# An S4D long convolution and a gMLP block on one core: inverse transforms in other matrix tiles, and a first phase in a new order

## Chip, cores and metric

One core of one Trainium2 chip. The metric is the device time of one execution in microseconds, the median of several runs.

## What is computed

The reference, cut to what matters (L = 2048 positions, D = 512 channels, N = 128 states a channel, Fh = 896):

```python
def _A_ref(u, log_A_real, A_imag, C_real, C_imag, log_dt, D_skip):
    dt = jnp.exp(log_dt)
    A = -jnp.exp(log_A_real) + 1j * A_imag
    C = (C_real + 1j * C_imag) * dt[:, None]
    P = jnp.exp((A * dt[:, None])[:, :, None] * pos[None, None, :])
    K = 2.0 * jnp.einsum("dn,dnl->dl", C, P).real
    y = irfft(rfft(u_t, 2 * L) * rfft(K, 2 * L)[None], 2 * L)[:, :, :L]
    return y.transpose(0, 2, 1) + u * D_skip[None, None, :]

def _B_ref(x, w_in, w_sp, b_sp, w_out):
    z = gelu(einsum("bsd,df->bsf", x, w_in))
    z1, z2 = z[..., :Fh], layernorm(z[..., Fh:])
    g = einsum("ts,bsf->btf", w_sp, z2) + b_sp[None, :, None]
    return einsum("bsf,fd->bsd", z1 * g, w_out)

h = x + _A_ref(layernorm(x), ...)
return h + _B_ref(layernorm(h), ...)
```

## The kernel before

The engines are TensorE (PE, with its weight loads as PEld), VectorE (DVE), ScalarE (ACT), GpSimd (POOL) and SyncE (SP), which issues most DMA transfers. A matmul in float32 shows as two records of MATMUL and two of LDWEIGHTS; "records" below are those of MATMUL.

**First phase (`phase_a`, 0 to 305 us of the span).** The channels are worked in four chunks of 128. `params` turns the parameters of a chunk into magnitudes and phases, on small tiles in buffers called `trio`; each phase is split in three parts that stand six rows above another six of them, and all rows of a chunk go to a scratch in HBM (`scr_stk`) in 16 stores of 16x6x128 a chunk. Four further rows of ones (`marks`) are written there once, by two transfers. `stack` reloads half a chunk as `sw` (512 KB), in the layout that TensorE needs. `unit` (8 a chunk) makes the kernel K of 16 channels: matmuls `c_k` x `sw` give all phases, ACT takes their sine, VectorE and GpSimd multiply them with powers (`f`, `wa`), and many small matmuls (`product`, 32x64 tiles) sum over the states into `ks`.

The long convolution is a transform of 4096 points in two stages, done as matmuls, for x and for K: `piece_a` and `piece_c` are the first stage (`st1`, 64x64 tiles, named `wb,big` and `wb,ks` in the profile), `piece_b` and `piece_d` the second (the matrix `a2`, shown as `big,a`); `piece_d` also multiplies the two spectra on VectorE; `exchange` swaps halves of partitions by DMA (`trio<-trio`). `piece_e` is the first stage of the inverse. For each of 4 channels it issues 8 matmuls with 64-column stationaries and 64 moving columns, 32 in a piece, 1024 in all; its result goes to `big`, with real and imaginary part on the two halves of the partitions.

The order of all this is written as tables. `RANKS` gives each operation its place, `FORMS` says for each operation that two engines could do which one does it (`evac`, the copy out of PSUM, is on ACT or VectorE), and `BANKS` gives each result its PSUM bank. All of it is recorded through one helper, so that every instruction of this phase has line 253. Within its engine an instruction waits behind whatever the table puts ahead of it; loads and stores stand in the same order on SP's queue.

**Second phase (`phase_b1`, 305 to 403 us).** It ends the inverse transform and begins the gMLP. `lines(n, g)` (matmul line 757) makes four lines of positions of quarter n, group g, as `y<-big,g`: 8 matmuls with 128 rows and 64 columns, two column tiles side by side, 16 groups in all. The matrix `g` is a constant of 2 MB. Group results of quarter 0 are added to x straight out of PSUM on VectorE (`add`, line 772), those of quarters 1 to 3 are first copied to a `stash` by ACT (`put_by`, line 764) and added later (line 769). `moments` (776), `centre` (matmul 785, called pm), `spread` (matmul 799, called pv), `scaled` (822 and 824), `turned` (831, 833) and `lower` (837) normalize and transpose 512 positions into `ht`; `by_halves` does that for quarter 0 in two halves; `column` (matmul 875) multiplies with `w_in`. `w1r` is `w_in` as loaded, split into high and low parts at 693 and 694. y, pz and the like share seven PSUM banks in turn; a new one waits until its bank's last content was copied away. The order on the engines is that of the calls at the end of the function.

**Afterwards** come the other half of `w_in` (`phase_b2`, 403 to 480 us) and the spatial product, the gate and the output (`phase_b3`, 480 to 839.7 us), which the change does not touch.

## Time and profile before

| | |
|---|---|
| median of 3 runs | 842.04 us (839.42 to 848.31) |
| the profiled execution | 841.47 us, span 839.7 |
| first phase | 0 to 305.14 us |
| last 512 records of `piece_e` | from 289.95 us |
| first y of the second phase | 305.78 us |
| DMA traffic | 121.22 MB, 144 GB/s on average |
| stores of `scr_stk`, reload of `sw` | 512.0 KB a reload, 8 reloads, 4.6 us to landing |

The span is the time between the first and the last record of the profile; the execution's own time is 1.8 us longer. A row of instructions names the line, the engine, the operation and output<-input, the shape, and how many. "Idle before" is time in which an engine waited, with the engine, tile and line that released it. Busy shares are averages over stages with different limits, so that the profile is read by stages: the busy time of each engine in a window, then the waits that end in it.

### The profile page before, as it was taken

How to read it: one execution, taken by the hardware profiler on the slowest of the kernel's cores; microseconds unless marked ns; L12 is line 12 of the kernel's file. 1: busy time of each engine (PE TensorE's matmuls, PEld its weight loads, DVE VectorE, ACT ScalarE, POOL GpSimd, SP SyncE). 2: the span in 40 equal slices, each digit the busy share in tenths (PEclk: the TensorE clock that was granted, in tenths of full speed). 3: DMA queues.
4: the chain of work that ended last, by engine and by line, in shares of the span. 5: the costliest groups of instructions: out<-in, count | busy, mean ns of one | idle time of the engine just before them, and what ended most of it. 6: DMA issues, size and time to landing. Idle time of an engine off the chain costs nothing.

```text
span 839.7 us, 22552 instructions
## 1 busy us (share of the span) xinstructions
PE 770.3 (92%) x9361; PEld 657.0 (78%) x9361; DVE 603.3 (72%) x1172; ACT 441.6 (53%) x778; POOL 285.1 (34%) x339
## 2 busy tenths in 40 slices
PE   1288898898898799999999999999999999999998
PEld 1157788787797699788999988888888888888887
DVE  7898597586676468764367689988956984888533
ACT  5889588688675145555224354466444443454111
POOL 4799599867745000000042100233231002232200
PEclk9999899899999999999999999999999999999999
DMA  9515442430505816545164044999799458799632
GB/s 339 159 36 156 119 103 70 110 84 26 129 4 108 335 19 174 139 138 188 39 151 125 1 139 140 193 231 219 186 207 214 156 148 203 159 246 243 153 110 79
DMA packets 70007, 121.22 MB, mean 144 GB/s; under 512 B 7569, under 2 KB 25105, under 8 KB 68881
## 3 DMA queue, kind: packets, MB, share of 16 engines
q1 hardware_dynamic: 58240, 98.28, 38.7%
q0 software_dynamic: 11664, 21.50, 15.6%
q8 instruction: 73, 1.20, 0.6%
q14 instruction: 30, 0.24, 0.1%
HBM read 90.40 MB, written 22.02 MB: 134 GB/s over the span
## 4 chain that ended last, share of the span: by engine, by line
PE 63%; DVE 1%; ACT 1%; issue 0%
PE m L1186 33%; PE pz L981 9%; PE pz L875 8%; PE po L1109 7%; PE pl L1109 2%; PE ps L253 2%; PE y L757 1%; DVE stats L776 0%; ACT w1r L824 0%; DVE xq L772 0%; ACT ht L833 0%; PE lnh_pm L785 0%; PE lnh_pv L799 0%; ACT zo L878 0%; ACT big L253 0%
## 5 line engine op out<-in xcount | busy, mean ns | idle before, releaser
L1186 PE MATMUL m<-wts,zc_wa 128*128 128x512 f32 x700 | 221.0, 395 | 0.0
L1186 PEld LDWEIGHTS m<-wts,zc_wa 128*128 128x128 f32 x700 | 131.7, 188 | 31.0
L1186 PE MATMUL m<-wts,zc_wb 128*128 128x512 f32 x350 | 138.0, 394 | 0.0
L1057 POOL DMA_DIRECT2D raws<-in_w_sp_dram x64 | 58.2, 1018 | 213.0 <-DMA raws<-in_w_sp_dram 212.2
L253 POOL TENSOR_TENSOR wa<-mt 128x512 f32<-128x512 f32 x96 | 107.2, 1138 | 26.8 <-PE ps L253 16.2
L693 ACT CAST wts<-raws 128x512 fp32r<-128x512 f32 x112 | 69.0, 619 | 47.6 <-DMA raws<-in_w_sp_dram 21.1
L694 DVE TENSOR_TENSOR wts<-raws,wts 128x512 fp32r<-128x512 f32 x112 | 76.7, 687 | 15.2 <-ACT wts L693 15.1
L1186 PEld LDWEIGHTS m<-wts,zc_wb 128*128 128x128 f32 x350 | 65.8, 188 | 15.6
L981 PE MATMUL pz<-w,ht 128*128 128x448 f32 x384 | 77.0, 362 | 0.0
L981 PEld LDWEIGHTS pz<-w,ht 128*128 128x128 f32 x384 | 72.0, 187 | 4.9
L875 PE MATMUL pz<-ht,w1h 128*128 128x512 f32 (+1 forms) x248 | 73.3, 376 | 0.1
L253 PE MATMUL ps<-c_inv,trio 128*64 128x64 f32 x2048 | 63.4, 224 | 3.2 <-DVE trio L253 2.2
L987 POOL TENSOR_SCALAR sm<-sm 128x1 f32<-128x1 f32 x16 | 5.6, 347 | 178.0 <-DVE sm L986 178.0
L253 PEld LDWEIGHTS ps<-c_inv,trio 128*64 128x64 f32 x2048 | 61.9, 140 | 4.8 <-DVE trio L253 2.6
L1109 PE MATMUL po<-w,gz 128*128 128x512 f32 x252 | 61.7, 392 | 0.0
L693 ACT CAST zc_wa<-raws 128x384 fp32r<-128x384 f32 (+1 forms) x70 | 37.1, 533 | 45.3 <-DVE raws L1091 24.3
L253 PE MATMUL ps<-big,a 128*128 128x128 f32 x448 | 56.1, 286 | 1.7 <-DVE trio L253 1.0
L253 PEld LDWEIGHTS ps<-big,a 128*128 128x128 f32 x448 | 54.5, 200 | 3.6 <-DVE trio L253 1.3
L1109 PEld LDWEIGHTS po<-w,gz 128*128 128x128 f32 x252 | 47.3, 188 | 10.7
L253 DVE TENSOR_TENSOR f<-ps,wa 128x512 f32<-128x512 f32 (+1 forms) x64 | 46.8, 750 | 8.6 <-ACT ps L253 4.1
L875 PEld LDWEIGHTS pz<-ht,w1h 128*128 128x128 f32 x248 | 45.1, 188 | 9.5 <-ACT ht L833 0.5
L253 DVE COPY big<-ps 128x512 f32<-128x512 f32 x39 | 26.1, 687 | 30.9 <-PE ps L253 30.8
(170 smaller groups left out, 1440.0 us busy)
## 6 DMA issues: line engine op xcount, KB each, us to landing
raws<-in_w_sp_dram SPq DMA_DIRECT2D x112, 256.0 KB, 4.0
raws<-in_w_sp_dram POOLq DMA_DIRECT2D x80, 256.0 KB, 5.9
trio<-trio SPq DMA_DIRECT2D x32, 256.0 KB, 3.8
scr_z<-zo SPq DMA_DIRECT2D x28, 256.0 KB, 2.0
big<-in_u_a_dram SPq DMA_DIRECT2D x8, 512.0 KB, 7.1
sw<-scr_stk SPq DMA_DIRECT2D x8, 512.0 KB, 4.6
xq<-in_u_b_dram SPq DMA_DIRECT2D x4, 1024.0 KB, 6.9
scr_h<-xq SPq DMA_DIRECT2D x16, 256.0 KB, 4.8
```

The source lines that it names most:

```text
L253: r = getattr(getattr(self.nc, e), method)(*map(self.real, args), **{k: self.real(x) for k, x in kw.items()})
L693: nc.scalar.copy(hi, src)
L694: nc.vector.tensor_sub(lo, src, hi.bitcast(F32))
L757: nc.tensor.matmul(ys[n, g][64 * h:64 * h + 64, i, :], gt[:, l0 + i], qv[:, h, l0 + i], start=True, stop=True, tile_position=(0, 64 * h))
L875: nc.tensor.matmul(pt[:, w], a[:, q, f], ht[n][k][:, q, w], start=((q, i) == terms[0]), stop=((q, i) == terms[-1]))
L981: nc.tensor.matmul(pt[:, :FQ], a[:, q], w2[:, b, q, f], start=(q == 0 and i == 0), stop=(q == 3 and i == 2))
L987: nc.gpsimd.tensor_scalar_add(sm[:, 14:15], sm[:, 13:14], 1e-5)
L1057: nc.gpsimd.dma_start(r, ws[1], accum_op=ALU.add)
L1109: nc.tensor.matmul(pt, gz[fb][x][:, P * a:P * a + P], wo[:, y, fb, w], start=(first and fb == fbs[0] and i == 0), stop=(last and fb == fbs ...
L1186: nc.tensor.matmul(pt, x[:, f], y, start=(k == 0 and i == 0), stop=(k == KT - 1 and i == 2))
```

## The change

1. `piece_e` uses stationaries of 128 columns and moves 128 columns: 2 matmuls for a channel, 8 a piece, 256 in all. Its result in `big` has the two halves of the points on the partitions and real and imaginary part along the free axis.
2. `lines` follows: it sums over real and imaginary part in two matmuls of 64x64 tiles, two groups at a time, 32 matmuls a pair of groups, 256 in all (128 before). In quarter 0 only the two tiles on the diagonal are used in turn; in quarters 1 to 3 all four, with even and odd lines on the two halves of the partitions. Rows of one half write a PSUM bank of their own. `g` becomes a constant of 4 MB in four pieces of 1 MB; two are loaded with the other early loads, two when the first phase's buffers are free.
3. `put_by` sorts even and odd lines with two copies of 64 partitions in place of one of 128: 24 copies, before 12. The calls of the second phase stand in a new order.
4. `stk` has the layout that the stores have, [4, 2, 64, 16, 128]: 4 stores a chunk in place of 16; `marks` takes four transfers; the reload reads runs of 512 bytes where it read 2 KB.
5. `RANKS`, `FORMS` and `BANKS` are new throughout the first phase. By engine: copies into `trio` go from 27 on ACT and 5 on VectorE to 18 and 14; the table loads on ACT from 15 to 20.

```diff
-    g = np.zeros((P, NL2, 64))
+    g = np.zeros((2, 64, NL2, 2, 64))
...
-        g[:, q] = np.einsum("ikl,qr->ikqrl", t, np.eye(2)).reshape(P, 64)
-    c["c_g"] = g.reshape(P, NL2 * 64)
+        g[:, :, q] = np.einsum("ikl,qr->kqirl", t, np.eye(2)).reshape(64, 2, 64)
+    c["c_g"] = g.reshape(P, NL2 * 128)
...
-    sws = [one(g1, f"sw{h}", [2, 4, NS]) for h in range(2)]
+    sws = [one(g1, f"sw{h}", [4, 2, NS]) for h in range(2)]
...
-    marks = stk_d.rearrange("c h (i r) s n -> (c h i) (r s n)", r=16)[:, 6 * 4 * NS:10 * 4 * NS]
-    for w in (slice(0, 32), slice(32, 128)):
-        nc.sync.dma_start(marks[w], cst["c_one"].to_broadcast([w.stop - w.start, 16 * NS]))
+    marks = stk_d.rearrange("c h p r n -> (c h p) r n")[:, 6:10]
+    for c in range(NCH):
+        nc.sync.dma_start(marks[P * c:P * c + P], cst["c_one"].rearrange("o (r n) -> o r n", r=4).to_broadcast([P, 4, NS]))
...
-            for su in range(SUC):
-                d = stk_d[c0 + c, su // 4].rearrange("(i r) s n -> s i r n", r=16)[su % 4]
+            for h in range(2):
                 for r in (0, 10):
-                    nc.sync.dma_start(d[:, r:r + 6], st6[16 * su:16 * su + 16, :, c, :])
+                    nc.sync.dma_start(stk_d[c0 + c, h, :, r:r + 6], st6[64 * h:64 * h + 64, :, c, :])
...
-        nc.sync.dma_start(sws[h], stk_d[c, h].rearrange("(a p) s n -> p a s n", a=2))
+        nc.sync.dma_start(sws[h], stk_d[c, h].rearrange("(s a i) r n -> (i r) s a n", s=4, a=2))
...
             for dd in range(4):
-                for h in range(2):
-                    for i, t in enumerate(spectra(c)[:2]):
-                        for r in range(2):
-                            nc.tensor.matmul(pt[64 * r:64 * r + 64, dd, 64 * h:64 * h + 64], t[:, 4 * s + dd, h],
-                                             c_inv[:, P * i + 64 * r:P * i + 64 * r + 64], start=(i == 0), stop=(i == 1),
-                                             tile_position=(0, 64 * r))
+                for i, t in enumerate(spectra(c)[:2]):
+                    nc.tensor.matmul(pt[:, dd, :], t[:, 4 * s + dd], c_inv[:, P * i:P * i + P], start=(i == 0), stop=(i == 1))
...
-    def lines(n, g, part=range(4)):
...
+    def lines(n, *groups):
+        for g in groups:
+            ys[n, g] = bank(f"y{n}_{g}", [P, 4, P])
+        if n == 0:
+            for turn in range(2):
+                for i in range(4):
+                    for r in range(2):
+                        for x, g in enumerate(groups):
+                            h, l = turn ^ x, 4 * g + i
+                            w = slice(64 * h, 64 * h + 64)
+                            nc.tensor.matmul(ys[n, g][w, i, :], gs[n][w, l, r], qv[w, r, l], start=(r == 0), stop=(r == 1),
+                                             tile_position=(64 * h, 64 * h))
+            return
+        for i in range(4):
+            for r in range(2):
+                for h, g in enumerate(groups):
+                    for odd in range(2):
+                        w, o, l = slice(64 * h, 64 * h + 64), 64 * odd, 4 * groups[0] + 2 * i + odd
+                        nc.tensor.matmul(ys[n, g][o:o + 64, i, :], gs[n][w, l, r], qv[w, r, 16 * n + l], start=(r == 0),
+                                         stop=(r == 1), tile_position=(64 * h, o))
+
+    for n, tag in ((2, "h21"), (3, "h11")):
+        gs.append(hp.tile([P, 16, 2, 64], F32, tag=tag, name=f"g{n}"))
+        load_g(n)
...
     def put_by(n, g):
-        o = stash[n][:, g].rearrange("p (l d x) -> p l d x", l=4, d=4)
-        nc.scalar.copy(o, ys[n, g].rearrange("p l (x d) -> p l d x", d=4))
+        h, y = g % 2, ys[n, g].rearrange("p l (x d) -> p l d x", d=4)
+        o = stash[n][:, g - h:g - h + 2].rearrange("p g (l d x) -> p (g l) d x", l=4, d=4)
+        for odd in range(2):
+            nc.scalar.copy(o[64 * h:64 * h + 64, odd::2], y[64 * odd:64 * odd + 64])
...
             scaled(n, 2 * h + 1)
-            if h:
-                put_by(2, 3)
             turned(n, 2 * h)
...
+            if h == 0:
+                put_by(2, 0)
+                put_by(2, 1)
...
-        lines(2, 0)
-        put_by(2, 0)
+        lines(2, 0, 1)
         add(1, 0)
         root(0, spread(0))
-        for n, g in ((2, 1), (2, 2), (2, 3), (3, 0)):
-            lines(n, g)
-        for g in range(1, 3):
-            put_by(2, g)
+        lines(2, 2, 3)
+        lines(3, 0, 1)
         by_halves(0)
         load_x(3)
-        for g in range(3):
-            put_by(3, g)
-            lines(3, g + 1)
-        for fb in range(3):
-            column(0, fb, A)
+        for n, g in ((2, 2), (2, 3), (3, 0), (3, 1)):
+            put_by(n, g)
+        column(0, 0, A)
+        column(0, 1, A)
+        lines(3, 2, 3)
+        column(0, 2, A)
+        put_by(3, 2)
         put_by(3, 3)
```

The tables show nothing to a reader, so here is what they and the calls make of the order at three places.

TensorE at the first chunk's units, before (`c_k,sw` are phases, `f0` and `wa` products, `wb,big` and `wb,ks` first stages of x and K, `trio,a2` a second stage):

```order
L253 MATMUL ps3_100<-trio_79,a2_78 128x64x2 x4
L253 MATMUL ps2_99<-wb_87,big_96 64x2x32 x16
L253 MATMUL ps0_97<-wb_87,big_96 64x2x32 x16
L253 MATMUL ps2_99<-c_k_88,sw1_90 128x512 x2
L253 MATMUL ps3_100<-f0_93 32x64 x16
L253 MATMUL ps0_97<-wb_87,ks0_80 64x2x32 x16
L253 MATMUL ps3_100<-wa_86,f0_93 32x64 x16
L253 MATMUL ps1_98<-wb_87,big_96 64x2x32 x16
L253 MATMUL ps0_97<-wb_87,ks1_81 64x2x32 x16
L253 MATMUL ps2_99<-wb_87,big_96 64x2x32 x16
L253 MATMUL ps1_98<-wb_87,ks4_84 64x2x32 x16
```

And the changed kernel at that place:

```order
L252 MATMUL ps2_99<-c_k_88,sw1_90 128x512 x2
L252 MATMUL ps0_97<-wb_87,big_96 64x2x32 x16
L252 MATMUL ps3_100<-trio_79,a2_78 128x64x2 x4
L252 MATMUL ps1_98<-wb_87,ks0_80 64x2x32 x16
L252 MATMUL ps0_97<-wb_87,big_96 64x2x32 x16
L252 MATMUL ps3_100<-trio_79,a2_78 128x64x2 x4
L252 MATMUL ps2_99<-wb_87,ks5_85 64x2x32 x16
L252 MATMUL ps0_97<-wb_87,big_96 64x2x32 x16
L252 MATMUL ps3_100<-trio_79,a2_78 128x64x2 x4
L252 MATMUL ps1_98<-wb_87,ks4_84 64x2x32 x16
```

The second stages stand between the small matmuls now, one to every two pieces, where before seven groups of small ones follow the phases without a break.

SP's queue at the start, before (`scr_stk` is the scratch, `sw` its reload, `a2` the matrix of 2 MB):

```order
L253 DMA a2_78<-in_c_a2_dram 128x4096
L253 DMA scr_stk<-in_c_one_dram 32x2048
L253 DMA scr_stk<-trio_79 16x6x128 x16
L253 DMA sw0_89<-scr_stk 128x2x512
L253 DMA wb_87<-in_c_f_dram 128x256
L253 DMA sw1_90<-scr_stk 128x2x512
L253 DMA big_96<-in_par2_dram 128x770
```

And the changed kernel's:

```order
L252 DMA scr_stk<-in_c_one_dram 128x512 x3
L252 DMA scr_stk<-trio_79 64x768 x4
L252 DMA sw0_89<-scr_stk 128x8x128
L252 DMA big_96<-in_par2_dram 128x770
L252 DMA wb_87<-in_skip_dram 128x128
L252 DMA c_inv_60<-in_c_inv_dram 128x256
L252 DMA wb_87<-in_c_f_dram 128x256
L252 DMA sw1_90<-scr_stk 128x8x128
L252 DMA scr_stk<-trio_79 64x768 x4
L252 DMA a2_78<-in_c_a2_dram 128x4096
```

Four stores stand in the place of sixteen, and a2 has gone from ahead of them to behind both reloads and the next chunk's stores.

ACT in the second phase, before (`stash2_4652<-y32_4764` is put_by of quarter 2, `w1r` the scaled positions, `ht` their transposed high part):

```order
L764 COPY stash2_4652<-y32_4764 128x512
L764 COPY stash2_4652<-y36_4790 128x512
L764 COPY stash2_4652<-y40_4799 128x512
L824 ACTIVATE w1r_4305<-xq0_4302,small_4647 128x128 x3
L833 CAST ht00_4788<-w1r_4305 128x4x128 x2
L824 ACTIVATE w1r_4305<-xq0_4302,small_4647 128x128 x4
L764 COPY stash2_4652<-y44_4808 128x512
L833 CAST ht00_4788<-w1r_4305 128x4x128 x2
L764 COPY stash3_4653<-y48_4817 128x512
```

And the changed kernel:

```order
L835 ACTIVATE w1r_3687<-xq0_3684,small_3834 128x128 x3
L844 CAST ht00_4071<-w1r_3687 128x4x128 x2
L775 COPY stash2_3843<-y2_0_4023 64x4x128 x2
L775 COPY stash2_3843<-y2_1_4024 64x4x128 x2
L835 ACTIVATE w1r_3687<-xq0_3684,small_3834 128x128 x4
L844 CAST ht00_4071<-w1r_3687 128x4x128 x2
L775 COPY stash2_3843<-y2_2_4073 64x4x128 x2
L775 COPY stash2_3843<-y2_3_4074 64x4x128 x2
L775 COPY stash3_3844<-y3_0_4107 64x4x128 x2
```

The copies of quarter 2 have gone from ahead of the scaling to behind its first casts, each as two.

More of the change, by code (lines that the diff above doesn't have):

```diff
@@ new lines @@
+    "1v1S1n0z0o1T1o1s1z191y1P1u201x171t1E152425292D2E2X2G2K2L2M2N2O2S2U2W2b2c2f2h2l2j2+363H3B2-3K2o2m2t3I2v303M4L3F3n4q6F4Y41"
+    "3b3u5X2y3V5C3T5n3z4I4V6C332x5V352e281m3m2B3w213t3k273G2V3S2p2q3v3r2u2i343D3q3i3l322T383s2R2r233x3y4243464O474A4B4C4E4M4N"
+    "4P4T4W4Z4g4i4k4j4l4o5D6B6T6M5u6m6Z6k5N6U4m6J6X5o574y6H5A686o6e6i5k6p6l4+586Y4p6n4n545B8O7P7Y9A9k1V222F2d373A3J3R1+2A262C"
+    "2I2J2Y2a2Z2g2k313E3N3P3c3o3p4D3j4b3a3g4s4t4x4w4v4u7D7O7k7q7w7x3U4K4J595g5-747m7s5K5R5d5p606s6z7A6+7B7N7S7X7y7p84888e958K"
@@ L122, in constants @@
     c["c_k"] = ck.reshape(P, 1024)
-    c["c_one"] = np.ones((1, 4 * 4 * NS))
+    c["c_one"] = np.ones((1, 4 * NS))
     lt = np.concatenate([
@@ L709, in phase_b1 @@
     w1r = xp.tile([P, 4, FH], F32, tag="w1r", name="w1r")
-    gt = xp.tile([P, NL2, 64], F32, tag="g", name="g")
+    gs = [xp.tile([P, 16, 2, 64], F32, tag=f"g{n}", name=f"g{n}") for n in range(2)]
     w1h = wp.tile([P, 4, FH], F32R, tag="wa", name="w1h")
     w1l = wp.tile([P, 4, FH], F32R, tag="wb", name="w1l")
-    qv = qt.rearrange("p c (h l x) -> p h l c x", h=2, l=NL2)
+    qv = qt.rearrange("p c (i l x) -> p i l c x", i=2, l=NL2)
     uv = ins["u_b"].rearrange("p (l x) -> p l x", x=P)
@@ L718, in load_x, with load_g @@
         nc.sync.dma_start(xqs[n % 3], uv[:, 16 * n:16 * n + 16])
-    def load_g(l0, n):
-        nc.sync.dma_start(gt[:, l0:l0 + n], cst["c_g"].rearrange("p (l m) -> p l m", m=64)[:, l0:l0 + n])
+    def load_g(n):
+        nc.sync.dma_start(gs[n], cst["c_g"].rearrange("p (n l i m) -> p n l i m", n=4, i=2, m=64)[:, n])
     load_x(0)
-    load_g(0, 16)
+    load_g(0)
     load_x(1)
-    load_g(16, 48)
+    load_g(1)
     for q in range(4):
@@ L749, in phase_b1 @@
     ys, norms, xbs = {}, {}, {}
-    def lines(n, g, part=range(4)):
-        l0 = 16 * n + 4 * g
-        if part[0] == 0:
-            ys[n, g] = bank(f"y{l0}", [P, 4, P])
-        for i in part:
-            for h in range(2):
-                nc.tensor.matmul(ys[n, g][64 * h:64 * h + 64, i, :], gt[:, l0 + i], qv[:, h, l0 + i], start=True, stop=True,
-                                 tile_position=(0, 64 * h))
+    def lines(n, *groups):
[21 more added lines that the diff above has]
+        load_g(n)
     stash = {n: hp.tile([P, 4, 512], F32, tag=t, name=f"stash{n}") for n, t in ((1, "h20"), (2, "h30"), (3, "h31"))}
     def put_by(n, g):
-        o = stash[n][:, g].rearrange("p (l d x) -> p l d x", l=4, d=4)
-        nc.scalar.copy(o, ys[n, g].rearrange("p l (x d) -> p l d x", d=4))
+        h, y = g % 2, ys[n, g].rearrange("p l (x d) -> p l d x", d=4)
+        o = stash[n][:, g - h:g - h + 2].rearrange("p g (l d x) -> p (g l) d x", l=4, d=4)
+        for odd in range(2):
+            nc.scalar.copy(o[64 * h:64 * h + 64, odd::2], y[64 * odd:64 * odd + 64])
     def add(n, g):
@@ L893, in phase_b1 @@
         for n in range(2):
-            for g in range(4):
-                lines(n, g)
+            for g in range(0, 4, 2):
+                lines(n, g, g + 1)
         for g in range(4):
```

58 lines of the change are left out of this document (26 added, 32 removed).

## The prediction

> **What bounds the kernel now.** First the page, for which engine works most and what ends last.
>
> ```profile
> span 839.7 us, 22552 instructions
> PE 770.3 (92%) x9361; PEld 657.0 (78%) x9361; DVE 603.3 (72%) x1172; ACT 441.6 (53%) x778; POOL 285.1 (34%) x339
> q8 instruction: 73, 1.20, 0.6%
> PE 63%; DVE 1%; ACT 1%; issue 0%
> ```
>
> TensorE works 92% of the span and carries the chain that ended last. The third row is a queue that fetches instructions: 73 packets and 1.20 MB, 16.4 KB each. TensorE has 2 x 9361 instructions (a matmul and its weight load), and 18722 / 73 is 256: this is TensorE's own program, arriving in blocks of 128 matmuls with their loads.
>
> Next the busy time by stage (window, its length, busy PE, PEld, DVE, ACT and POOL with the count of records, then the granted TensorE clock, DMA share and GB/s).
>
> ```profile
> 0.00:305.14 305.14, 240.18 (x6760) 212.59 (x6760) 220.13 (x397) 212.72 (x337) 201.31 (x227) 0.97 0.42 122
> 305.14:403.00 97.86, 97.06 (x660) 82.60 (x661) 63.60 (x197) 51.20 (x101) 0.00 (x0) 1.00 0.51 146
> 480.00:839.70 359.70, 356.01 (x1558) 289.68 (x1556) 269.88 (x489) 153.28 (x295) 63.81 (x74) 1.00 0.72 177
> 80.00:100.00 20.00, 13.50 (x509) 12.04 (x498) 8.75 (x17) 10.88 (x14) 10.64 (x13) 0.84 0.65 162
> 260.00:280.00 20.00, 13.46 (x532) 11.91 (x529) 8.51 (x13) 7.31 (x12) 6.84 (x10) 0.91 0.77 202
> ```
>
> Behind 305 us TensorE has no gap: what is added there is added to the time. In the first phase it is idle for 305.14 - 240.18 = 65 us, so what matters there is which idle time the change removes, not which work. Two slices stand out: in 80 to 100 and 260 to 280 all engines are idle together, under the highest DMA shares. The view of waits and TensorE's timeline say why (waits: total, times, longest; timeline: start, length, records, idle before).
>
> ```profile
> PE ps L253 <- issue: 21.6, 18, 3.2
> 84.11 1.01 PE L253 MATMUL ps<-wb,big 64*64 64x64 f32 x27 [2.69 <-issue]
> ...
> 90.66 0.28 PE L253 MATMUL ps<-wb,ks 64*64 64x64 f32 x3
> 92.46 2.08 PE L253 MATMUL ps<-wb,ks 64*64 64x64 f32 x125 [1.53 <-issue]
> 94.41 0.33 PE L253 MATMUL ps<-wb,big 64*64 64x64 f32 x3
> 96.34 0.68 PE L253 MATMUL ps<-wb,big 64*64 64x64 f32 x29 [1.60 <-issue]
> ...
> 275.26 0.43 PE L253 MATMUL ps<-f 128*32 128x64 f32 x7 [3.18 <-issue]
> ```
>
> Eighteen times TensorE waited for nothing that the profile shows, 21.6 us in all. Between the stall before 92.46 and the next there are 125 + 3 = 128 matmuls, one block of the fetch queue. They took 96.34 - 1.60 - 92.46 = 2.28 us, and the next block came 3.88 us after the last. I read these stalls as a fetch that cannot follow: a block comes about every 3.9 us under such DMA traffic, and a block whose 128 matmuls need less is waited for.
>
> **The change, part by part.** Prices are the rows of the first phase by form (busy total, mean ns of one, which overlaps its neighbours, so the cost of one is total over count).
>
> ```profile
> L253 PE MATMUL ps<-c_inv,trio 128*64 128x64 f32 x2048 | 63.4, 224 | 3.2 <-DVE trio L253 2.2 <-issue 0.9
> L253 PE MATMUL ps<-big,a 128*128 128x128 f32 x448 | 56.1, 286 | 1.7 <-DVE trio L253 1.0 <-ACT big L253 0.7
> L253 PE MATMUL ps<-wb,ks 64*64 64x64 f32 x1024 | 23.3, 230 | 10.2 <-issue 9.4 <-ACT big L253 0.8
> L253 DVE COPY trio<-ps 128x512 f32<-128x512 f32 x6 | 4.1, 686 | 0.4 <-PE ps L253 0.2
> L253 ACT ACT_TABLE_LOAD x15 | 19.2, 1283 | 1.0 <-PEq L1292 0.7
> 289.95 15.18 PE ps L253 x512
> ```
>
> *First inverse stage, work.* 2048 records of 31 ns (63.4 / 2048) become 512 of the 128x128 kind at 125 ns (56.1 / 448): 64 us against 63. The array's time stays. The last chunk, which nothing covers (last row, 512 records), becomes 128 x 115 to 125 ns = 14.7 to 16.0 against 15.18; bounds -1 and +2, taken -0.4.
>
> *Fetch.* What changes is the number of instructions: 1536 matmuls fewer, 12 blocks of 128. Cutting both orders of instructions into blocks and pricing each by these rows, I count 19 blocks under 3.6 us in 53 before, and 10 in 41 after, most of them now alone between long ones, because the order sets transforms of 125 ns a matmul between the cheap ones (23 ns: 23.3 / 1024). Taking the stall as proportional: 21.6 x 9 / 19 = 10.2 us less. Bounds: 4, if only the stalls of isolated blocks go (a run of three cheap blocks remains ahead of the second phase, where the slice of 260 to 280 shows the heaviest traffic), and 21.6, if all go. Taken -10.2.
>
> *Clock.* The granted clock is 0.84 and 0.91 in the two slices with the stalls. If the clock falls because of the pauses, half of what the two slices lose (13.50 x 0.16 + 13.46 x 0.09 = 3.4 us) comes back: -1.5, between 0 and -3.4.
>
> *Startup.* The parameters' way through HBM sets when the first products can begin.
>
> ```profile
> 17.33 9.85 SPq L253 DMA_DIRECT2D scr_stk<-trio  x16
> 29.45 0.29 DVE L253 SCALAR_TENSOR_TENSOR trio<-ps,trio 128x128 f32<-128x128 f32 x1 [2.23 <-DMA scr_stk<-trio]
> 33.31 2.05 PE L253 MATMUL ps<-c_k,sw 128*128 128x512 f32 x4
> 39.95 1.81 DVE L253 TENSOR_TENSOR f<-ps,wa 128x1024 f32<-128x1024 f32 x2
> 0.00:40.00 40.00, 8.91 (x27) 6.20 (x27) 32.12 (x151) 27.33 (x61) 25.27 (x34) 1.00 0.75 260
> ```
>
> SP issues sixteen stores in 9.85 us; four take a quarter, 2.5, so 7.4 us of the way is gone, and the 2 MB load a2, which stood ahead of the stores, now stands behind them and both reloads. But VectorE is busy 32.12 of the first 40 us, so the gain ends where VectorE becomes the limit: the half of the small norms that moves behind the first unit's products takes some 4.5 us of small operations (0.2 to 0.3 us each, like the one in the second row) out ahead of them, and the one wait that goes is the 2.23 us of that row, of which the order lets me count only part, as other parameters still arrive when they did. I take -3.5; bounds 0 (VectorE as late as before) and -7.4. The reload in runs of 512 bytes where they were 2 KB could give back a microsecond or two; it is inside the bounds.
>
> *Evictions move.* Nine copies go from ACT to VectorE: 9 x 0.686 = 6.2 us on VectorE; five table loads more are 5 x 1.283 = 6.4 us on ACT. Neither engine is full (220 and 213 of 305 us), and TensorE's idle time covers most: +1, between 0 and +6.
>
> *Second inverse stage.* It lies behind 305 us, where all counts.
>
> ```profile
> 305.78 7.21 PE L757 MATMUL y<-big,g 128*64 128x128 f32 x128 [0.69 <-ACT big L253]
> 306.93 0.69 DVE L772 TENSOR_TENSOR xq<-y,xq 128x512 f32<-128x512 f32 x1 [3.23 <-PE y L757]
> 308.44 0.67 DVE L772 TENSOR_TENSOR xq<-y,xq 128x512 f32<-128x512 f32 x1
> 313.07 0.62 PE L785 MATMUL lnh_pm<-stats,c_mean 128*128 128x16 f32 x4
> 319.30 1.21 ACT L833 CAST ht<-w1r 128x512 fp32r<-128x512 f32 x2 [0.35 <-DVE w1r L831]
> 321.52 8.75 PE pz L875 x72
> 324.04 2.04 ACT L764 COPY stash<-y 128x512 f32<-128x512 f32 x4
> 330.11 0.51 PE L785 MATMUL lnh_pm<-stats,c_mean 128*128 128x16 f32 x4
> L764 ACT COPY stash<-y 128x512 f32<-128x512 f32 x12 | 6.7, 588 | 6.4 <-PE y L757 5.3 <-DMA scr_h<-xq 1.1
> ```
>
> A record of y costs 7.21 / 128 = 56 ns with two tiles at work. The first quarter doubles its records (64 to 128) and still has two tiles at a time: 7.2 us against 3.6, +3.6. The other three double theirs (192 to 384) with four tiles: at 28 ns they cost 10.75 us as before. That 28 is an estimate; the nearest row with four tiles is wb,ks at 23 ns with half the columns, and the other end is 56. Then the waits, counted from the first y at 305.78. VectorE's first add starts at 1.15 and its period is 1.5 (308.44 - 306.93); now a pair of groups ends together, at 3.6. The first pm stood at 7.3; it now stands behind 7.2 + 3.6 = 10.8 us of y. The casts that open the column begin at 13.5 and end at 14.7, 7.4 behind the pm; now 10.8 + 7.4 + 0.7 (the pv waits for a pair of groups, 1.8 us, not one group, 1.1) = 18.9. TensorE has 2 x 0.6 + 5.4 us of work for these 8.1: 1.5 idle. Two columns of 24 (8.75 / 3 = 2.9 each) then last to 24.7. The last pair of lines, now behind them, needs the bank that put_by(2,2) empties. ACT reaches it late: the four stash copies that began at 18.3 (324.04) begin 4.2 later with the casts, and 2.2 later again because put_by(2,0) and put_by(2,1), four half copies, now stand in between, at 0.55 each (0.51 by the row at 324.04, 0.588 by the mean; a half copy is taken at the price of a whole one); two more half copies make it 25.8. TensorE is idle for 1.1, with everything of the columns queued behind. Pair and third column end at 30.5, while VectorE's adds and moments, started by the late casts, reach the second pm at 30.9 where it was 24.3. So 3.6 + 1.5 + 1.1 + 0.4 = +6.6, and 0.4 for three blocks of y that at 28 ns last 3.6 us, less than the fetch's 3.9: +7.0. Bounds: +3.6 (all waits covered) and +14 (twice the waits, or the 2 MB of g that now load behind 305 us, in two pieces of the 1 MB that took 6.9 us for xq by the page's DMA issues, come after the lines at 10.8 and 15.6).
>
> ```profile
> xq<-in_u_b_dram SPq DMA_DIRECT2D x4, 1024.0 KB, 6.9
> ```
>
> **Sum.** -3.5 - 10.2 - 1.5 - 0.4 + 1 + 7.0 = -7.6 on the profiled 841.47: **834**. The median shown, 842.04, is 0.6 above that execution, well inside its runs.
>
> **Rivals.** (1) *The stalls go wholly.* The blocks that remain cheap are isolated, and one long block ahead lets the queue run ahead. For it: no stall stands inside the last 512 records of c_inv, 3.8 us a block. Against it: the run of three cheap blocks. All 21.6 instead of 10.2 and 3 of clock: 841.47 - 3.5 - 21.6 - 3 - 0.4 + 1 + 7 = 821.
>
> (2) *The four tiles do not run side by side in y* (slower). Each 64x64 matmul with 128 columns costs the 56 ns of the diagonal pair; 384 records cost 21.5 us, 10.75 more, all behind 305 us: 834 + 10.75 = 845. It decides from 28 + 7600 / 384 = 48 ns a record. For it: the two-tile row is the only measured one with 128 columns. Against it: wb,ks at 23 ns.
>
> The Trainium skill, in TensorEngine Tiling (Array Packing), Key Properties, says that different tiles run loads and matmuls in parallel; the 23 ns row agrees, and by it this rival falls.
>
> (3) *Fetch is not the cause of the idle time called issue*, so fewer instructions save nothing: the stalls and the clock stay, 834 + 10.2 + 1.5 = 846, slower. For it: stalls coincide with DMA bursts, which the change keeps. Against it: their distance of exactly 128 matmuls.
>
> The Trainium skill, in Runtime: NRT & Kernel Launch, Instruction fetch mechanics, states this rival as a rule: instructions come in 16 KiB blocks of 256, and crossing a block's edge is mostly hidden because dispatch is slower than the fill. The block's size agrees with the 16.4 KB of this trace; that it is hidden does not, by the 21.6 us.
>
> **How the numbers follow.** Forecast 45%, rival 1 22%, rival 2 16%, rival 3 17%. 1% (8.4 us) is about what a measurement of this kernel can tell from no change. The forecast at 834 lies on that edge: faster 20, same 22.5, slower 2.5. Rival 1 gives 21 and 1. Rivals 2 and 3 at 845 and 846 are half same, half slower when their other terms are at their bounds: 18 same, 15 slower. Together faster 0.41, same 0.41, slower 0.18. The range, 819 to 850, reaches from rival 1 to rivals 2 and 3 with some of their bounds; the forecast's own is 826 to 842.
>
> **What would show it.** Right: some 1536 fewer TensorE records in the first phase and its instruction packets down from 73 to about 60; idle time called issue near 11 us; first products near 36 us instead of 39.95; the first pm 10.8 us behind the first y, the second 31; y records at 56 and then 28 ns. Wrong if: the issue stalls stay above 17 us or vanish; y of the last three quarters costs over 40 ns a record; VectorE's first products come no earlier; or a new wait of TensorE on VectorE's copies of trio appears in the first phase.

## The result, and the profile after

The changed kernel takes **854.0 us** (median of 12 runs, 849.52 to 858.39), the kernel before in the same sessions 844.46 (12 runs, 839.42 to 849.12): a ratio of 1.0105, 95% interval 1.0073 to 1.0138. The forecast was 834, from 819 to 850. The profiled execution took 850.38, 8.9 more than that of before.

The page of the changed kernel (busy time by engine, the fetch queue):

```profile
span 848.4 us, 19968 instructions
PE 772.8 (91%) x8081; PEld 658.5 (78%) x8081; DVE 620.0 (73%) x1187; ACT 449.1 (53%) x785; POOL 281.5 (33%) x334
q8 instruction: 63, 1.03, 0.5%
```

Fewer records, as meant: 1280 fewer on TensorE and 10 fewer packets of instructions. To see where the time went, the span is cut at 80 us, at the first y and at the second pm. Windows of the kernel before, which answer the question how much TensorE worked in each (window, length, then busy PE first):

```profile
40.00:60.00 20.00, 15.91 (x462) 11.42 (x462) 19.08 (x26) 16.95 (x37) 17.43 (x22) 1.00 0.03 8
60.00:80.00 20.00, 18.31 (x429) 14.98 (x428) 18.78 (x29) 19.73 (x40) 18.96 (x26) 1.00 0.52 158
40.00:305.78 265.78, 231.28 (x6733) 206.39 (x6733) 188.02 (x248) 186.01 (x279) 176.04 (x193) 0.97 0.36 101
```

and of the changed kernel:

```profile
0.00:40.00 40.00, 6.26 (x17) 3.85 (x17) 32.40 (x119) 21.91 (x50) 19.77 (x26) 1.00 0.61 198
40.00:60.00 20.00, 11.65 (x180) 8.29 (x184) 19.48 (x47) 17.60 (x32) 14.68 (x19) 1.00 0.41 107
60.00:80.00 20.00, 15.88 (x453) 12.75 (x447) 15.33 (x22) 16.69 (x35) 16.06 (x20) 0.91 0.40 131
40.00:302.70 262.70, 229.62 (x5207) 204.12 (x5207) 204.71 (x294) 192.35 (x285) 178.18 (x197) 0.98 0.40 115
```

| stretch | before | changed | difference |
|---|---|---|---|
| TensorE idle until 80 us | 80 - (8.91 + 15.91 + 18.31) = 36.9 | 80 - (6.26 + 11.65 + 15.88) = 46.2 | +9.3 |
| idle from 80 us to the first y | 28.7 | 20.6 | -8.1 |
| busy until the first y | 240.2 | 235.9 | -4.3 |
| first y stands at | 305.78 | 302.70 | -3.1 |
| first y to second pm | 24.33 | 35.86 | +11.5 |
| second pm to the end | 509.6 | 509.8 | +0.2 |

So in these two profiles the first phase gained 3.1 us where 14.6 were forecast, and the second lost 11.5 where 7.0 were. TensorE's idle time ahead of the first y did not fall: it is 36.9 + 28.7 = 65.6 us before and 46.2 + 20.6 = 66.8 changed. What fell is the busy time, and that moves with the clock of one execution: in the control run below the same program is busy for 240.3 us up to its first y.

The start, in rows of several engines' timelines of the changed kernel:

```profile
0.73 0.66 SPq L252 DMA_DIRECT2D scr_stk<-in_c_one_dram  x1
1.44 0.57 SPq L252 DMA_DIRECT2D trio<-in_par_dram  x1
7.08 0.23 DVE L252 TENSOR_SCALAR trio<-trio 128x128 int32<-128x128 int32 x1 [6.18 <-DMA trio<-in_par_dram]
20.50 4.49 SPq L252 DMA_DIRECT2D scr_stk<-trio  x4
31.28 0.39 SPq L252 DMA_DIRECT2D sw<-scr_stk  x1
43.93 1.80 DVE L252 TENSOR_TENSOR f<-ps,wa 128x1024 f32<-128x1024 f32 x2
56.90 1.20 DVE L252 TENSOR_TENSOR big<-big,ps 128x1024 f32<-128x1024 f32 x1
59.16 0.67 DVE L252 SCALAR_TENSOR_TENSOR f<-wa,ps 128x512 f32<-128x512 f32 x1
```

A marks transfer now stands first on SP's queue, ahead of the parameters. They arrive when VectorE begins on them, at 7.08 us; in the kernel before that was here:

```profile
3.27 0.23 DVE L253 TENSOR_SCALAR trio<-trio 128x128 int32<-128x128 int32 x1 [2.35 <-DMA trio<-in_par_dram]
49.89 0.68 DVE L253 SCALAR_TENSOR_TENSOR f<-wa,ps 128x512 f32<-128x512 f32 x1
```

The 3.8 us go through to the first f (43.93, was 39.95). The four stores are issued in 4.49 us, not 9.85, but the reload waits 6.3 us behind them where it waited 1.7. By its place in the timeline the postponed half of the norms is the next delay: it stands on VectorE ahead of the third unit (the row at 56.90 is its end), whose f comes 9.3 us later than before.

TensorE's waits in the first phase of the changed kernel, and its timeline in the last chunk and the second phase:

```profile
PE ps L252 <- issue: 6.8, 8, 1.9
PE ps L252 <- DMA wa<-scr_xhat: 4.0, 2, 3.6
```

```profile
284.98 14.40 PE L252 MATMUL ps<-c_inv,trio 128*128 128x128 f32 x112 [3.37 <-DVE trio L252]
299.98 2.05 PE L252 MATMUL ps<-c_inv,trio 128*128 128x128 f32 x16 [0.60 <-DVE big L252]
302.70 7.09 PE L755 MATMUL y<-big,g 64*64 64x128 f32 x125 [0.68 <-ACT big L252]
309.69 3.71 PE L763 MATMUL y<-big,g 64*64 64x128 f32 x126
313.33 0.62 PE L796 MATMUL lnh_pm<-stats,c_mean 128*128 128x16 f32 x4
321.71 0.39 PE L887 MATMUL pz<-ht,w1h 128*128 128x256 f32 x1 [1.65 <-ACT ht L844]
328.37 3.68 PE L763 MATMUL y<-big,g 64*64 64x128 f32 x60 [3.18 <-ACT stash L775]
338.56 0.51 PE L796 MATMUL lnh_pm<-stats,c_mean 128*128 128x16 f32 x4
```

The stalls called issue fell from 21.6 to 6.8 us. A new wait of 3.6 us on a load of x came. The last chunk's c_inv takes 17.05 us with a pause in it, where it took 15.18. In the second phase y costs 57 ns a record in the first quarter and 29 with four tiles, and the first pm and the column stand 10.6 and 19.0 us behind the first y. Then TensorE stands still for 3.2 us, and the next 60 records cost 61 ns each. The windows say why (granted clock third from the end):

```profile
324.75:328.37 3.62, 0.44 (x6) 0.20 (x5) 3.25 (x6) 3.40 (x8) 0.00 (x0) 0.80 0.43 127
328.37:330.35 1.98, 1.98 (x38) 1.98 (x42) 1.98 (x8) 1.93 (x4) 0.00 (x0) 0.50 0.72 302
```

Behind the pause the clock is halved, until 333.5 us by narrower windows.

### The profile page after: what moved, and what is told of

Its sections match the earlier page's. It is cut to its first block, busy times and chain, and to the rows that moved or that the text cites. A ratio compares the mean times of both kernels' runs of the same rounds, so it can differ in the third digit from the quotient of the medians.

```text
span 848.4 us, 19968 instructions
## 1 busy us (share of the span) xinstructions
PE 772.8 (91%) x8081; PEld 658.5 (78%) x8081; DVE 620.0 (73%) x1187; ACT 449.1 (53%) x785; POOL 281.5 (33%) x334
## 4 chain that ended last, share of the span: by engine, by line
PE 63%; ACT 2%; DVE 1%; issue 0%; DVEq 0%; ACTq 0%
PE m L1197 33%; PE pz L992 9%; PE pz L887 8%; PE po L1120 7%; PE pl L1120 2%; PE ps L252 2%; PE y L763 1%; PE y L755 1%; ACT w1r L835 1%; ACT ht L844 0%; ACT stash L775 0%; PE lnh_pv L810 0%; PE lnh_pm L796 0%; DVE w1r L842 0%; DVE w1r L833 0%
## 5 line engine op out<-in xcount | busy, mean ns | idle before, releaser
L252 PE MATMUL ps<-c_inv,trio 128*128 128x128 f32 x512 | 62.3, 284 | 4.2 <-DVE trio L252 3.4
L252 PEld LDWEIGHTS ps<-c_inv,trio 128*128 128x128 f32 x512 | 60.6, 198 | 5.8 <-DVE trio L252 3.6
L252 PEld LDWEIGHTS ps<-big,a 128*128 128x128 f32 x448 | 52.1, 191 | 3.5 <-ACT big L252 0.9
L687 ACT CAST zc_wa<-z 128x128 fp32r<-128x128 f32 (+2 forms) x56 | 23.7, 431 | 43.0 <-PE m L1197 35.9
```

The source lines that it names most:

```text
L252: r = getattr(getattr(self.nc, e), method)(*map(self.real, args), **{k: self.real(x) for k, x in kw.items()})
L687: nc.scalar.copy(hi, src)
```

## Experiments

A job's kernels run on one chip beside the kernel before; ratios are to that, with 95% intervals.

**Marks behind the parameters.** The first marks transfer gets a place beside the other three.

```diff
...
+        m = sorted(self.marks, key=lambda o: o["rank"])
+        m[0]["rank"] = m[1]["rank"] - 0.5
         return sorted(self.ops, key=lambda o: o["rank"])
...
```

> The changed kernel, with the one marks transfer that stands first on SP's queue put next to the other three, behind the parameters. Theory: this transfer of 256 KB is why the first parameters land at 7.1 us instead of 3.3, and the whole chain to the first products is late by it. Then VectorE's first parameter operation comes at 3.3 to 3.9 us, the first f at about 40 instead of 43.9, and the time falls by 3 to 4 us. Rival: the startup ends with VectorE and with the reload behind four long stores; then the parameters land early all the same, but the first f moves by less than 1 us and the time by less than 1.

850.62 us, ratio 1.0107 (1.0077 to 1.0138).

```profile
3.30 0.23 DVE L255 TENSOR_SCALAR trio<-trio 128x128 int32<-128x128 int32 x1 [2.40 <-DMA trio<-in_par_dram]
40.31 1.80 DVE L255 TENSOR_TENSOR f<-ps,wa 128x1024 f32<-128x1024 f32 x2
302.00 7.09 PE L759 MATMUL y<-big,g 64*64 64x128 f32 x125 [0.68 <-ACT big L255]
```

The step moved as the theory of the late parameters has it: first operation at 3.30, first f 3.6 us earlier. But the first y is 0.7 earlier and the time is that of the changed kernel. The lead, followed along the units in both traces, is 3.6 us at the start, 3.2 at about 140 us, 1.6 at 240, and gone by 268. The start was slow for the reason named; it was not, by itself, the loss.

**Copies of quarter 2 earlier.** They move from behind the first casts to behind `lines(3, 0, 1)`.

```diff
-            if h == 0:
-                put_by(2, 0)
-                put_by(2, 1)
...
         lines(3, 0, 1)
+        put_by(2, 0)
+        put_by(2, 1)
         by_halves(0)
```

> The changed kernel, with put_by(2,0) and put_by(2,1) called ahead of by_halves(0) and not inside it. Theory: the four half copies on ACT hold up the bank that the last pair of lines needs; TensorE then stands still for 3.6 us and its clock is halved for 5.6 us behind that. Then the pause falls from 3.2 us to about 1.2, the granted clock stays at 1.00, y of the last pair costs 28 ns a record and not 60, the second pm comes 5 us earlier (near 31 us behind the first y, where it is 35.9) and the time falls by 4 to 6 us. Rival: the slow y has nothing to do with the pause (the DMA traffic there, or the tiles waiting for each other's banks); then y stays near 60 ns and the time falls by 2 us.

851.2 us, ratio 1.0106 (1.0063 to 1.0149). Timeline row of the last pair of lines, and a window around it:

```profile
332.31 1.96 PE L763 MATMUL y<-big,g 64*64 64x128 f32 x60 [1.36 <-ACT stash L775]
```

```profile
331.50:334.50 3.00, 2.19 (x62) 2.02 (x63) 3.00 (x10) 2.92 (x6) 0.00 (x0) 1.00 0.59 242
```

The pause is 1.36 us where it was 3.18, the clock stays at 1.00, and the same 60 records take 1.96 us, not 3.68. The second pm comes 340.00 - 308.48 = 31.5 us behind the first y (35.9 before the mend). So 4.3 us of this stage were the place of four copies. The median does not show them: the first phase, whose code is that of the changed kernel, happened to end 5.8 us later in this profile.

**The inverse stage in small tiles again**, with all the rest of the change.

```diff
-                for i, t in enumerate(spectra(c)[:2]):
-                    nc.tensor.matmul(pt[:, dd, :], t[:, 4 * s + dd], c_inv[:, P * i:P * i + P], start=(i == 0), stop=(i == 1))
+                for r in range(2):
+                    for i, t in enumerate(spectra(c)[:2]):
+                        for h in range(2):
+                            nc.tensor.matmul(pt[64 * h:64 * h + 64, dd, 64 * r:64 * r + 64], t[:, 4 * s + dd, h],
+                                             c_inv[:, P * i + 64 * r:P * i + 64 * r + 64], start=(i == 0), stop=(i == 1),
+                                             tile_position=(0, 64 * h))
```

> The changed kernel, with each 128x128 matmul of the first inverse stage cut into four of 64 columns and 64 moving columns, the numbers of instructions of the kernel before; all else is the changed kernel's. Theory: the pauses called issue are TensorE's instruction fetch, so 1536 more matmuls bring them back from 6.8 us to 13 to 22 us, the fetch packets go from 63 to about 75, and the time grows by 6 to 14 us. Rival: the pauses went because the order is another one; then they stay under 9 us and the time within 2.

862.31 us, ratio 1.0248 (1.0207 to 1.029), some 11 us above the two kernels before it. Its waits and its fetch queue:

```profile
PE ps L252 <- issue: 14.6, 15, 3.0
```

```profile
q8 instruction: 75, 1.23, 0.6%
```

Twelve packets more, 7.8 us of the waits called issue more, and the time follows with some 11 us; the other 3 us are not traced. Work on the array is the same by the prices of both forms. This settles the fetch step: fewer instructions do remove these waits, and the rival that they don't is out.

**Filler work in the pauses.** Twelve matmuls into an unused bank, ahead of the last chunk's c_inv and ahead of the last pair of lines.

```diff
+        o["calls"] = [self.fill] * 12 + o["calls"]
...
         column(0, 1, A)
+        fill = tp("fill", [P, 512])[:, :P]
+        for _ in range(12):
+            nc.tensor.matmul(fill, c_mean, c_mean, start=True, stop=True)
         lines(3, 2, 3)
```

> The changed kernel with two times 12 matmuls of constants added (results unused), in the two pauses of over 3 us: ahead of the last chunk's first inverse stage and ahead of the last pair of lines. Theory: the pause halves the clock for some 5 us afterwards; filled, the granted clock stays at 1.00, the last chunk's c_inv costs 115 to 118 ns a record and not 129, y of the last pair 28 ns and not 60, and the time falls by 4 to 5 us although work is added. Rival: the slow matmuls behind the pauses come from DMA traffic or from the operands; then they stay slow and the time does not fall.

850.86 us, ratio 1.0108 (1.0081 to 1.0136).

```profile
286.20 12.71 PE L255 MATMUL ps<-c_inv,trio 128*128 128x128 f32 x112
327.89 1.96 PE L769 MATMUL y<-big,g 64*64 64x128 f32 x60 [0.50 <-ACT stash L781]
```

With a busy array the same 60 records of y take 33 ns each where they took 61, as they do with the copies moved. So the slow records behind this pause are the clock, not their operands. That repeats over all profiles of this document: in the six with the pause of 3.2 us these records cost 47 to 61 ns, in the eight without it 33. The second pm stands 33.4 us behind the first y. In the time nothing is resolved.

For c_inv this run decides nothing. A record costs 113 ns here, where 14.40 / 112 = 129 in the changed kernel; but in the first experiment, without filler and behind the same pause, it cost 12.80 / 112 = 114:

```profile
285.88 12.80 PE L255 MATMUL ps<-c_inv,trio 128*128 128x128 f32 x112 [3.37 <-DVE trio L255]
```

**The changed kernel once more**, on another chip, as a control for the next three.

> The changed kernel once more, beside the next three on one chip. Theory and rival alike: 1.0% slower than the kernel before; its profile shows how far the same program's stages move from one execution to another.

853.68 us, ratio 1.0116 (1.0076 to 1.0157).

```profile
309.19 7.09 PE L755 MATMUL y<-big,g 64*64 64x128 f32 x125 [0.68 <-ACT big L252]
```

```profile
0.00:309.19 309.19, 240.25 (x5225) 212.27 (x5225) 237.42 (x412) 214.61 (x334) 197.95 (x222) 0.96 0.43 124
```

The same program's first y stands at 309.19 here, at 302.70 in the profile above; up to there the mean clock is 0.96 here and 0.98 there, and TensorE is idle for 309.19 - 240.25 = 68.9 us here. Differences of a few microseconds between single profiles of the first phase therefore prove nothing by themselves; the second phase agrees (second pm 35.9 behind the first y in both).

**Only the new matrix tiles.** Layout of `stk` and the three tables of before; the two inverse stages and the second phase of the changed kernel.

```diff
-        nc.sync.dma_start(sws[h], stk_d[c, h].rearrange("(s a i) r n -> (i r) s a n", s=4, a=2))
+        nc.sync.dma_start(sws[h], stk_d[c, h].rearrange("(a p) s n -> p a s n", a=2))
...
-                    nc.sync.dma_start(stk_d[c0 + c, h, :, r:r + 6], st6[64 * h:64 * h + 64, :, c, :])
+                    nc.sync.dma_start(d[:, r:r + 6], st6[16 * su:16 * su + 16, :, c, :])
```

> The kernel before with only the two inverse stages changed (first stage in 128-column matmuls, second in 64x64 tiles, with g, put_by and the order of the second phase); the tables of order and the layout of the parameters' scratch are the old ones. Theory: the loss is in the startup (the new first transfer), behind the first phase (the second phase's order) and not in the fewer instructions: the pauses called issue fall from 21.6 us to 8 to 12, the first f stays at 40 us, the first y comes 6 to 10 us earlier than 305.8, the second phase loses the same 11 to 12 us, and the time is 1 to 5 us above the kernel before. Rival: the gain in the first phase came from the new order alone; then issue stays at 17 to 22 us, the first y near 305, and the time is 9 to 12 us above.

845.95 us, ratio 1.0015 (0.9988 to 1.0043): 8 us less than the control. It was run again:

> The kernel before with the inverse stages alone, once more, for a second profile of its first phase: the first one was of an execution at the upper end of its runs, with a mean granted clock of 0.979. Theory: at a clock near 0.99 its first y comes at 295 to 299 us (before 305.8, changed kernel 302.7). Rival: it comes near 303 again, and the 8 us between this kernel and the changed one do not lie in the first phase.

845.87 us, ratio 1.0043 (1.0011 to 1.0075). Waits of TensorE in the kernel before, then in this one:

```profile
PE ps L253 <- issue: 21.6, 18, 3.2
PE ps L253 <- DVE trio L253: 16.5, 8, 6.4
PE ps L253 <- DVE f L253: 0.8, 3, 0.4
```

```profile
PE ps L253 <- issue: 17.0, 11, 3.4
PE ps L253 <- DVE trio L253: 16.9, 8, 6.2
PE ps L253 <- DVE f L253: 0.9, 3, 0.4
PE ps L253 <- DMA wa<-scr_xhat: 0.3, 1, 0.3
```

and in the changed kernel, beside the issue waits of 6.8 and the x load's 4.0 shown above:

```profile
PE ps L252 <- DVE trio L252: 21.7, 8, 7.4
PE ps L252 <- DVE f L252: 4.5, 3, 2.7
```

In this second run the tiles alone take 4.6 us off the issue waits and leave the others nearly as they were (in the first run issue is 15.3 us and `trio` 19.0). Both runs missed what was expected of them: issue waits of 8 to 12 us, and a first y well ahead of the changed kernel's. It stands at 302.95 and 302.84 us, beside 302.70; but these two executions lie 3.9 us above the median of their kernel, and that of the changed kernel lies 3.6 us below its own.

The new tables take off 10 more, and add 4.8 on VectorE's `trio`, 3.6 on `f` and 3.7 on the x load: what they win from the fetch they lose to VectorE and SP. These rows add up to 2 us and not to 8, so they show what is traded, not the whole loss.

That the loss lies in the first phase is seen when all profiles are put side by side, without the one with the small tiles. VectorE's last operation on `f` starts at 260.0 to 263.0 us in the six with the old tables and at 267.9 to 272.7 in the seven with the new ones. Among those without filler, TensorE is idle for 60.5 to 63.7 us ahead of the first y with the old tables (five profiles) and for 64.0 to 68.9 with the new ones (six). Here is the last f before, in this second run, and in the second run of the tiles with the mended second phase (below):

```profile
270.14 0.68 DVE L253 SCALAR_TENSOR_TENSOR f<-wa,ps 128x512 f32<-128x512 f32 x1
```

```profile
262.52 0.68 DVE L253 SCALAR_TENSOR_TENSOR f<-wa,ps 128x512 f32<-128x512 f32 x1
```

```profile
260.02 0.68 DVE L253 SCALAR_TENSOR_TENSOR f<-wa,ps 128x512 f32<-128x512 f32 x1
```

**Marks and second phase mended, new tables.** The edit of the first experiment, that of the second, and `column(0, 2, A)` ahead of `lines(3, 2, 3)`.

```diff
         column(0, 1, A)
-        lines(3, 2, 3)
         column(0, 2, A)
+        lines(3, 2, 3)
```

> The changed kernel with three mends: the first marks transfer behind the parameters, put_by(2,0) and put_by(2,1) ahead of by_halves(0), and column(0,2,A) ahead of lines(3,2,3). Theory: the two places that lost time give it back and keep it: first f at 40 us, second pm 29 to 31 us behind the first y, no pause of over 2 us in the second phase, 7 to 9 us less than the changed kernel, within 0.3% of the kernel before. Rival: what the start gives is taken back by pauses later in the first phase, as far as the last chunk; then 3 to 5 us less than the changed kernel, and still 0.4 to 0.8% slower than before.

849.84 us, ratio 1.0054 (1.0023 to 1.0085), beside the control's 1.0116: 3.8 us less than the control, where 7 to 9 were expected. First f at 40.38, second pm 334.30 - 302.99 = 31.3 behind the first y, as meant; half of the two gains together arrives. The wait on the x load has grown to 4.9 us: part of the start's gain ends there.

**The tiles and the mended second phase, old tables.**

> The kernel before with the two inverse stages changed, and with the same two mends of the second phase's order. Theory: fewer instructions help and only the second phase's order costs: 5 to 6 us less than with the inverse stages alone, 0 to 6 us below the kernel before. Rival (fewer instructions give nothing by themselves): 3 to 7 us above the kernel before.

841.36 us, ratio 0.996 (0.9936 to 0.9985). Against the kernel with the new tables beside it, 849.84, this is 8.5 us less, with intervals apart. Again:

> The same kernel as in the run of that edit (old tables and old scratch, changed inverse stages, the second phase's order mended), once more on another chip. If its lead is real: 0.2 to 0.7% below the kernel before again. If it was the spread of that job: within 0.2% or above.

842.16 us, ratio 1.0012 (0.9984 to 1.0039): the lead over the kernel before is not confirmed. In both jobs it is 3.7 to 4.6 us below the same kernel with the unmended second phase, as the stage in the traces has it (second pm 31.3 behind the first y, not 34.9).

**x loads among the stores.** On the marks and second phase mended, two of the x loads that stand behind eight long stores on SP's queue go between them. In this kernel these two loads fill their tiles before the old contents were read, so that part of the convolution is made from other data, with the same amount of work.

```diff
+        late[0]["rank"], late[1]["rank"] = st[2]["rank"] - 0.5, st[4]["rank"] - 0.5
```

> The changed kernel with the three mends of the run before it (marks, put_by, columns) and a fourth: the two loads of x that stand behind the eight long stores of the parameters on SP's queue are put among them, behind the second and the fourth. Theory: what the earlier start gains is lost at about 139 us, where TensorE waits 3.6 to 4.9 us for such a load, whose issue stands behind 6.8 us of stores; then that wait falls under 1 us, the products behind it keep a lead of 5 us or more over the changed kernel, and the time is 2 to 4 us below the three mends alone, within 0.3% of the kernel before. Rival: another wait takes its place there (the reload behind the stores, or the units that VectorE feeds); then the lead shrinks all the same and the time stays as with three mends, 0.4 to 0.6% above before.

847.14 us, ratio 1.008 (1.0054 to 1.0107).

```profile
132.50 1.14 PE L258 MATMUL ps<-wb,wa 64*64 64x64 f32 x32 [6.10 <-DMA wa<-scr_xhat]
```

The wait did not go; another of 6.1 us stands there. So it is not shown that the stores ahead of the load caused the wait, and which place on SP's queue would be right is not settled by this run.

**The new layout of `stk` on the old tables**, with the mended second phase: four stores for sixteen, at the first, second, ninth and tenth of the sixteen places.

```diff
+            ranks[i:i + 16] = [ranks[i], ranks[i + 1], ranks[i + 8], ranks[i + 9]]
```

> The kernel before with the two inverse stages changed, the two mends of the second phase's order, and now also the parameters' scratch in the changed layout: 4 stores a chunk, four marks transfers, runs of 512 bytes in the reload, at the places that the old tables give them. The forecast's term: 7 us of issue go, the reload is issued at about 22 us and not 29, and the first f comes 2 to 7 us earlier. The trace's reading of the changed kernel: the four stores need as much longer to land as they are issued sooner (6.2 us of wait behind 4.5 us of issue, where it was 1.5 behind 9.85), so the reload is issued at 27 to 29 us, the first f moves by less than 1.5 us, and the time stays within 0.3% of the same kernel with the old layout.

842.02 us, ratio 1.001 (0.9987 to 1.0033).

```profile
24.27 0.40 SPq L260 DMA_DIRECT2D sw<-scr_stk  x1
39.24 1.81 DVE L260 TENSOR_TENSOR f<-ps,wa 128x1024 f32<-128x1024 f32 x2
```

The reload is issued at 24.27, where the two runs of the old layout had 28.70 and 28.29 and where 27 to 29 were expected: here the four stores keep what they gain in issue, so the longer wait behind them in the changed kernel does not come from the layout alone. The first f comes at 39.24, where those two runs had 40.56 and 39.33. Four microseconds on the queue are worth about one or none: VectorE sets the start. The first experiment agrees, where the reload was issued at 31.10, as late as in the changed kernel (31.28), and the first f still came 3.6 us earlier. The layout costs nothing that this run can tell. So the 8 us are in the three tables, or in these tables together with the new layout; the tables were not tried without it.

**Eight filler matmuls ahead of the last chunk's c_inv**, on the tiles with the old tables and the mended second phase.

```diff
+        o["calls"] = [self.fill] * 8 + o["calls"]
```

> The kernel before with the changed inverse stages and the mended order of the second phase (842.2 to 841.4 us in two jobs, the kernel before 842.3 to 843.7), with 8 matmuls of constants added (results unused) in the pause of 2.2 us ahead of the last chunk's inverse stage. Theory: that pause keeps the clock down; filled, the last 128 records of c_inv cost 114 to 118 ns each where they cost 134 in three of four profiles, and the time is 1 to 3 us lower, below the kernel before by 0.1 to 0.5%. Rival: the clock was lowered by the fetch pauses and the DMA burst before it, between 260 and 280 us; then c_inv stays at 134 ns in this profile and the time does not move.

840.71 us, ratio 0.9964 (0.9942 to 0.9986).

```profile
284.28 14.56 PE L256 MATMUL ps<-c_inv,trio 128*128 128x128 f32 x128 [0.21 <-DVE trio L256]
```

A record costs 14.56 / 128 = 114 ns, where the two runs of the tiles with the old tables had 17.27 and 17.20 / 128 = 134, and the clock is 1.00 from 280 to 300 us. But the profile of the kernel without filler and with the new `stk` shows 14.56 as well, behind a pause of 2.24 us, so that the filler is not shown to be the cause: the clock behind such a pause is low in some executions only. In the second run of the tiles it was at 0.73 within the pause already. This version beats the kernel before by its interval, by 3 us of 844, and the changed kernel by some 13 across jobs. The lead of its base did not come a second time, and this one was run in one job only.

## Why the prediction was wrong, point by point

*Startup, -3.5 forecast, bounds 0 to -7.4.* Wrong in sign: 9.3 us more idle time by 80 us. The steps that failed: the order of SP's queue was read around the stores and not at its head, where the first marks transfer delays the parameters by 3.8 us (shown by moving it). The issue of the stores fell by 5.4 us, not by the 7.4 costed (4.49 us, not 2.5), and the reload then waited 4.6 us longer for them to land. That wait is not the layout's alone: on the old tables, where one marks transfer stands ahead of the stores and not four, it was 4.2 us behind 2.90 of issue. And even there the way through the queue was worth a microsecond or none, as VectorE sets the start. Of the small norms that move behind the first unit's products I costed what it saves ahead of them, not what comes late next: the third unit's f, 59.16 for 49.89. That this order on VectorE is the cause is argued from the timeline; it was not tried alone.

*Fetch, -10.2.* The mechanism was right: 10 packets fewer, and issue waits of 6.8 us where 11.4 were forecast; taking the small tiles back costs 11 us. Where only the tiles change, the last f comes 7.6 us earlier and in another kernel 10.1, which is the size forecast, though the issue waits themselves are only 3.8 to 6.3 us lower in the six profiles of the tiles with the old tables. The Trainium skill, in Runtime: NRT & Kernel Launch, Instruction fetch mechanics, calls the crossing of a block's edge mostly hidden; the run with the small tiles contradicts that for this kernel, by its 7.8 us.

*Evictions, +1, bounds 0 to +6.* Mis-sized. VectorE is not full, as I argued, but it is late where it is waited for: waits on its `trio` and `f` grow by 5.2 and 3.7 us, 8.9 together. Whether the nine copies or the new order around them cause this was not separated. A share of busy time over 305 us does not price a wait. The x load behind eight stores on SP, 4.0 us, was in no term.

*Clock, -1.5.* Not resolved: up to the first y the mean clock is 0.97 before, 0.98 in the profile above and 0.96 in the control. (Half of the 3.4 us counted is 1.7, not 1.5.) A term for new pauses was missing: behind 3.2 us of standing still the clock was 0.50. The Trainium skill, in TensorE: Matmul & The Clock Gate, Part 1: The HAM clock gate, puts the halved clock behind at least one idle window of about 3.4 us and says that the window runs freely. The trace differs in the length: the clock fell behind pauses of 3.2 us in all six profiles that have one there, and behind 3.37 us ahead of c_inv in some executions and not in others. No run here shows the window itself.

*Last chunk, -0.4, bounds -1 and +2.* +1.9: 17.05 us for 15.18, at 129 ns a record behind a pause of 3.4 us and with a wait of 0.6 on VectorE. The upper bound held.

*Second inverse stage, +7.0, bounds to +14.* +11.5. Most of the steps stood: y at 57 and 29 ns (56 and 28), the first pm at 10.6 (10.8), the column at 19.0 (18.9), the bank free at 328.37 - 302.70 = 25.7 (25.8). Rival 2 falls by the 29 ns. The step that failed is the length of the columns. I took three columns of 24 records from a row of 72; that row held six half columns, so that what stands ahead of the last pair is 12 records a column. The columns were over 2 us sooner than costed, and the pause 3.2 us, not 1.1. At that length it also took the clock: 3.68 us for 60 records in place of 1.96. With the calls mended the stage costs 31.3 - 24.3 = 7.0; that this is the figure forecast is chance, since the order of the columns is another there.

*The sum.* Of the 16.4 us between 834 and the profiled 850.4, the first phase brought 11.5 and the second inverse stage 4.5. Four of the six terms were too good (startup, evictions, last chunk, second inverse stage), all but the last chunk by something that stood late behind the thing I looked at. Rivals 2 and 3 end nearest (845 and 846), and both are out as mechanisms; no rival had the time for its own reason. Of the first phase's new order I had one rival too few: that it trades waits on the fetch for waits on VectorE and SP.

*Open:* which moves in the tables cost most of the 8 us, since the waits shown account for 2 of them; why the reload waits longer behind four stores in the changed kernel; where on SP's queue the x loads belong; and whether the DMA bursts or the pauses of the fetch lower the clock between 260 and 280 us.

## What to carry to other kernels

Fewer and larger instructions can pay through the fetch even where the array's time is the same; but when an order is changed for it, follow every operation put later to whoever waits for it next, and look at the head of each DMA queue. A pause of TensorE of about 3 us may have to be priced twice, once for itself and once for the records behind it at a lower clock; ahead of the last pair of lines, twelve matmuls of filler or four copies placed earlier removed the second price. And profiles of single executions are compared in rows that hold over all of them, such as idle time or the place of one operation, not by one difference of a few microseconds.

## What the runs showed that was not expected

- Executions of one program differ with the granted clock, without an edit: the first y of the changed kernel stood at 302.70 and 309.19 us, at mean clocks of 0.98 and 0.96. In one job, 29 runs of the kernel before reached from 839.96 to 849.72 us.
- One 256 KB store from a repeated row of ones at the head of the queue made the next load 3.8 us later.
- Four stores in place of sixteen were issued in 5.4 us less and waited for 4.6 us longer in the changed kernel; on the old tables the reload behind them came 4 us earlier.
- The same pause of 3.37 us ahead of c_inv was followed by 114 ns a record in one profile and by 129 to 138 in five others.
- Two 64x64 tiles on the diagonal cost 57 ns a record of 128 columns in float32, four tiles 29.
